# First-layer eviction as tanh(h/2) under activation tables that also hold arctan or sine, with every step handed over in a new order

## The chip, the cores and the metric

The kernel runs on one core of one Trainium2 chip. The metric is the device time of one execution in microseconds (us). The core has five engines that run side by side and wait for one another through semaphores: TensorE (PE, with its weight loads as PEld), VectorE (DVE), ScalarE (ACT), GpSimd (POOL) and SyncE (SP), which here only issues DMAs. Each engine works through its own list of instructions in the order in which the program handed them over; an instruction that waits holds back all that stand behind it on its engine.

## The reference

Three layers follow one another. The first is a linear recurrence with decay over 768 steps (4 batches, 8 heads, head size 48), the second a feed-forward layer with the activation h·tanh(softplus(h)), the third eight experts with a greedy assignment of 3072 tokens.

```python
for t in range(S):                       # recurrence
    cur = einsum('bhd,bhe->bhde', u * kt, vt)
    y[:, :, t] = einsum('bhd,bhde->bhe', rt, state + cur)
    state = wt[..., None] * state + einsum('bhd,bhe->bhde', kt, vt)
...
h = x @ w_in                             # 384 -> 2048
g = h * tanh(log1p(exp(h)))
x = g @ w_out                            # 2048 -> 384
...
logits = x @ w_gate                      # greedy: best (token, expert) first, 384 tokens each
h = maximum(x[mask] @ w1[e], 0.0); out[mask] = h @ w2[e]
```

The kernel uses that, with s = sigmoid(−h), tanh(softplus(h)) = sin(pi/2 − 2·arctan(s)): first s, then its arctan, then a sine with scale −2 and bias pi/2.

## The kernel before, in words

The first two layers run interleaved, in 12 groups of 256 tokens. Two attention units (128 tokens each; 24 in all, numbered n) make the input `xg` of one group. Group g of the second layer has eight slots: slot t (96 in all, 8g to 8g+7) is one `mm1`, 18 matmuls into one of two PSUM buffers `Hp`, followed by its eviction on ScalarE (L579, into `es`) and a scaled copy of h (L348, into `hs`; L348 is the helper `move` when it goes to ScalarE, L346 when it goes to VectorE). After four slots, half a group H = 2g or 2g+1 is complete: `act_ln` takes the arctan of the half in one instruction (L588), `act_sin` the sine in two (L597), `act_he` multiplies by h on VectorE (L605), and `act_g` writes the result as a high and a low f16 part (the high by `move`, the low on VectorE, L622). The second matmul, `mm2` (L636), takes g from there; it runs as one stream of 384 steps of three matmuls for the 12 groups, far behind `mm1`, and `CFG["rate"]` and `CFG["beat"]` say how many steps are handed over at each slot. When a tile's 16 steps end, `put_x1` takes it out of PSUM and a DMA writes it away.

An attention unit has ten steps: `att0` (a running product on VectorE and a product `rk`), `att_inv` (Ln and Exp on ScalarE, L376 and L377), `att1` and `att1b` (four products on VectorE, L384 to L416), `bon1` and `bon2` (small matmuls, their evictions, and `Dt`), `att_K` (transposes and the copy `kn`), `att_A` (64 small matmuls), `att_S` (the state; L467 and L472 to L476) and `att4` (the output y: 32 matmuls, the high part of `xg` by `move`, the low part on VectorE, L496). After the second unit of a group, six DMAs on SyncE's queue (L502) bring the last rows of `xg` in place.

The weights of the second layer are converted from f64 to two f16 halves by the kernel itself in the first 16 slots (`conv` and `split`, VectorE and ScalarE; `og_T` and `og_M` fold the gate's weights in). After the last slot come the gate (VectorE, with the rest of the `mm2` stream as filler on TensorE) and the experts.

The order is written out by hand. Every step is put on a list with a key (`at(key, step)`); the list is sorted by key and handed over in that order, and each engine works in that order. Slot t has key t + `CFG["mm1"]`; the steps of a unit have keys `8*(n//2) - 8` plus the offsets of `CFG["u"]`. `CFG["dve"]` says which of the movable instructions go to VectorE. The functions of ScalarE belong to named sets of tables, and the trace has a load (ACT_TABLE_LOAD, 1283 ns) wherever the next function is of another set; copies run without one. `natural_log_exp_and_others` (Ln and Exp) is loaded before `att_inv` and `trig_and_small` (arctan and sine) before the arctan and sine of both halves of a group, each by a call; the load for the sigmoid of the next eviction is put in by the framework. In groups 1 to 10 ("both" in the code), the Ln and Exp of two units, the arctan of the odd half and all four sines stand one behind another at the start of the next group, ahead of that group's first eviction.

Of the kernel before, what the change touches and what calls it, by code (L numbers as in the profile page):

```python
# [18 lines left out]
P = 128  # L19
# [4 lines left out]
CFG = {'conv': [-27.9, -26.2, -0.2, 0.8, 1.8, 2.8, 3.7, 5.3, 5.9, 6.6, 7.3, 8.0, 8.7, 10.4, 10.6, 11.3],  # L24
 'split': [-27.3, -25.6, 0.9, 1.9, 2.9, 3.8, 4.7, 5.6, 6.7, 7.4, 8.1, 8.8, 9.0, 11.2, 11.4, 12.1],
 'ogT': [7.4, 8.45, 9.9, 10.25, 10.95, 11.85, 12.55, 12.75],
 'ogM': [8.15, 9.35, 10.2, 10.9, 11.35, 11.95, 12.75, 13.95],
 'u': ({'att0': -5.0, 'bon1': -3.1, 'bon2': -2.1, 'inv': 0.1, 'r1': 0.101, 'k1': 0.102, 'K': 1.28, 'A1': 1.3,
        'S': 2.39, 'y': 2.4},
       {'att0': -2.8, 'bon1': -1.9, 'bon2': -0.8, 'inv': 0.11, 'r1': 0.111, 'k1': 0.112, 'K': 3.3, 'A1': 3.4,  # L30
        'S': 4.59, 'y': 4.6}),
 'un': {0: {'att0': -17.25,
            'inv': -16.75,
            'r1': -16.55,
            'bon1': -15.85,
            'k1': -16.37,
            'K': -16.05,
            'A1': -15.25,
            'bon2': -15.45,
            'S': -15.75,  # L40
            'y': -13.75},
        1: {'att0': -20.15,
            'inv': -20.14,
            'r1': -19.9,
            'bon1': -19.0,
            'k1': -19.4,
            'K': -17.4,
            'A1': -17.4,
            'bon2': -18.5,
            'S': -17.0,  # L50
            'y': -17.15},
        2: {'att0': -19,
            'inv': -18.99,
            'r1': -18.9,
            'bon1': -17.98,
            'k1': -18.85,
            'bon2': 4.5,
            'K': 5.3,
            'A1': 5.5,
            'S': 5.5,  # L60
            'y': 7.4},
        3: {'att0': -22.95,
            'inv': -22.8,
            'r1': -17.6,
            'bon1': 2.3,
            'k1': -17,
            'bon2': 3.05,
            'K': 3.85,
            'A1': 4.2,
            'S': 4.05,  # L70
            'y': 6.5},
        4: {'K': 4.96,
            'A1': 4.82,
            'S': 6.99,
            'y': 7.0,
            'att0': -0.0,
            'bon1': 0.87,
            'bon2': 3.15,
            'inv': 2.57,
            'r1': 2.6,  # L80
            'k1': 3.2},
        5: {'y': 7.46,
            'att0': -1.5,
            'bon1': 2.0,
            'bon2': 4.6,
            'inv': 3.67,
            'r1': 3.7,
            'k1': 4.3,
            'K': 5.9,
            'A1': 6.2,  # L90
            'S': 7.45},
        6: {'att0': -3.6, 'bon1': -2.7, 'bon2': -0.9},
        7: {'att0': -1.4, 'bon1': -0.6, 'bon2': -0.4}},
 'rate': [(9, 0), (16, 19), (80, 195), (82, 200), (85, 216), (89, 218), (93, 234), (99, 258)],
 'beat': (16, 80, (5, 3, 2, 2, 2, 2, 1, 5)),
 'close_cv': 15.0,
 'close_att': 86.65,
 'mm1': 0.7,
 'mm2': 1.275,
 'aln': -0.1,  # L100
 'tanh': (1.475, 1.66),
 'g': (3.0, 3.0725),
 'both': ((0.12, (0.14, 0.15), (1.33, 2.75)), (0.13, (2.45, 2.5), (3.6, 4.7))),
 'begin': {('warm', 0): -32,
           ('wg',): 5.6,
           ('ld', 4): -23.99,
           ('ld', 5): -25.98,
           ('ld', 6): -23.8,
           ('ld', 7): -21.7,
           ('ld', 8): -23.6,  # L110
           ('ld', 9): -23.6,
           ('warm', 1): -25.1,
           ('warm', 2): -24.4,
           ('warm', 3): 0.15,
           ('warm', 4): 5.65,
           ('warm', 5): 7.15,
           ('warm', 6): 9.9},
 'warm': [36, 12, 18, 12, 12, 0, 12],
 'amount': {'I0': 3, 'I1': 0, 'g': 1, 't': 6, 'c': 3, 'o': 11},
 'dve': {'lg': set(),  # L120
         'glo': {0,
# [51 lines left out]
         'ghi': {2} | {i for i in range(4, 46) if i % 4 != 3},  # L173
         'hs': set(),
         'rk': {0, 1, 2, 3, 5, 6, 7, 9, 10, 11, 12, 13, 14, 15, 16, 17, 18, 19, 20, 21, 22, 23},
         'x0': set(),
         'bT': {22},
         'wT': {4}},
 'nd0': 8,
 'lg2': 5.2,  # L180
 'alone': {9},
 'lg': 4.9,
# [4 lines left out]
def tile_rwkv_mish_greedy_moe(  # L187
# [111 lines left out]
    nc.scalar.preload_act_table_set("natural_log_exp_and_others")  # L299
# [9 lines left out]
    nc.vector.memset(right, math.pi / 2)  # L309

# [42 lines left out]
    def warm(n):  # L353
        if n:
            wps = pq.tile([P, 512], F32, name="Y", bufs=2)
        for _ in range(n):
            nc.tensor.matmul(wps, id16, warm_rhs, start=True, stop=True)
# [13 lines left out]
    def att_inv(n):  # L371
        need(("att0", n))
        inv = pa.tile([P, 2 * NP, L], F32, name="inv", bufs=2)
        if n > 1 and (n < 6 or n % 2 == 0):
            nc.scalar.preload_act_table_set("natural_log_exp_and_others")
# [22 lines left out]
    def bon2(n):  # L398
        pb = pq.tile([P, C], F32, name="Y", bufs=2)
        nc.tensor.transpose(pb, bTs.pop(n), ident)  # L400
# [21 lines left out]
    def att_A(n):  # L422
        c = UN[n][1]
        need(("k1", n), *([("S", n - 1)] if c else []))
        made.add(("A", n))
        k1, r1, _ = st[n]
# [16 lines left out]
    def att_K(n):  # L443
        need(("k1", n))
        k1, r1, _ = st[n]
        if UN[n][1] + 1 < NCH:
            t = pq.tile([P, NP, C], F32, name="Y", bufs=2)
            for p in range(NP):
                nc.tensor.transpose(t[:, p, :], k1[:, p, :], ident)
# [132 lines left out]
    def act_ln(H_):  # L582
# [3 lines left out]
        if H_ % 2 and 0 < H_ // 2 < NG - 1:  # L586
            nc.scalar.preload_act_table_set("trig_and_small")
# [739 lines left out]
```

## Time and profile before

| | |
|---|---|
| time, median of 3 runs | 871.36 us (871.22 to 871.53) |
| the profiled execution's own time | 869.97 us |
| its span, first to last instruction | 868.3 us |
| TensorE matmuls busy | 757.0 us, 87% of the span |
| VectorE / ScalarE / GpSimd busy | 542.5 / 456.4 / 63.8 us |
| mean granted clock of TensorE | 0.965 of full speed |
| loads of function tables on ScalarE | 44, 1283 ns each |

The profile lists, for each stretch or instruction, when it began, how long it took, the engine, the line of the kernel, and in brackets how long the engine had stood idle before it and what ended that. `x18` counts instructions merged into one row. A matmul's duration holds a tail that overlaps the next one; the distance from one row's start to the next is what it costs TensorE.

### The profile page before, as it was taken

The page shows a single profiled execution, that of the slowest core. Times are in us where ns is not written, and L with a number is a line of the kernel's source. Part 1 is how long each engine was busy: PE and PEld are TensorE (multiplying, and loading weights), DVE is VectorE, ACT ScalarE, POOL GpSimd, SP SyncE. Part 2 cuts the span into 40 slices and gives each one's busy share as a digit, 9 for nine tenths or more (in the row PEclk, how much of TensorE's full clock was granted, in tenths as well). Part 3 has the DMA queues.
Part 4 walks back from the last instruction along what each step waited for, and adds up shares of the span by engine and source line. Part 5 has one row for each costly group of instructions (what it writes and reads, how often), then busy time and mean ns, then how long its engine had stood idle before and what let it go on. Part 6 is the DMA issues. An engine that isn't in the chain of part 4 may idle for free. (4 is left out here: it accounts for less than half of the span.)

```text
span 868.3 us, 20153 instructions
## 1 busy us (share of the span) xinstructions
PE 757.0 (87%) x8819; PEld 521.7 (60%) x8819; DVE 542.5 (62%) x949; ACT 456.4 (53%) x682; POOL 63.8 (7%) x102
## 2 busy tenths in 40 slices
PE   6763879898989989898898878999959999999996
PEld 3452656676767767676676656555536566555564
DVE  7699884958668584967667243577765433555520
ACT  2358885775848666674748376411005543455521
POOL 1000000000000000000000001000011331222311
PEclk9797899999999999999999999999979999999999
DMA  7860512304121240322200000400144445554200
GB/s 281 246 187 14 147 37 53 75 14 89 40 59 39 52 83 6 88 49 52 45 18 11 15 10 11 164 20 20 30 160 147 145 143 182 191 191 166 79 29 28
DMA packets 22220, 74.12 MB, mean 85 GB/s; under 512 B 4496, under 2 KB 13072, under 8 KB 20080
## 3 DMA queue, kind: packets, MB, share of 16 engines
q1 hardware_dynamic: 19056, 63.35, 25.1%
q0 software_dynamic: 3072, 9.44, 3.4%
q8 instruction: 71, 1.16, 0.6%
q14 instruction: 21, 0.17, 0.1%
HBM read 62.15 MB, written 9.44 MB: 82 GB/s over the span
## 5 line engine op out<-in xcount | busy, mean ns | idle before, releaser
L576 PE MATMUL Hp<-xg,wi 128*128 128x256 f16 x1728 | 211.3, 278 | 12.4 <-ACT hs L348 10.7
L636 PE MATMUL X<-wo,g 128*128 128x392 f16 (+1 forms) x1152 | 214.6, 330 | 0.5 <-ACT wT L348 0.5
L576 PEld LDWEIGHTS <-wi 128*128 128x128 f16 x1728 | 169.1, 100 | 42.9 <-issue 11.1
L636 PEld LDWEIGHTS <-g 128*128 128x128 f16 x1152 | 107.5, 99 | 64.1 <-issue 1.7
L579 ACT ACTIVATE es<-Hp 128x512 f32<-128x512 f32 x96 | 57.4, 598 | 131.0 <-PE Hp L576 130.9
L1172 PE MATMUL Hp<-xe,a 128*128 128x384 f16 (+1 forms) x612 | 100.8, 316 | 6.5 <-DVE hT L1177 5.2
L1189 PE MATMUL X<-a,hT 128*128 128x384 f16 x576 | 97.2, 326 | 0.0
L1172 PEld LDWEIGHTS <-a 128*128 128x128 f16 x612 | 57.6, 98 | 48.3 <-issue 14.4
L1189 PEld LDWEIGHTS <-hT 128*128 128x128 f16 x576 | 56.4, 98 | 34.8
L605 DVE TENSOR_TENSOR hs<-hs,es 128x1024 f32<-128x1024 f32 x48 | 56.7, 1220 | 29.8 <-ACT es L597 29.8
L622 DVE TENSOR_TENSOR g<-hs,g 128x1024 f16<-128x1024 f32 x48 | 58.6, 1225 | 22.4 <-ACT g L348 21.3
L1177 DVE SCALAR_TENSOR_TENSOR hT<-Hp,hT 128x384 f16<-128x384 f32 x64 | 35.4, 554 | 46.8 <-ACT hT L1176 46.8
L1118 DVE SCALAR_TENSOR_TENSOR a<-stg,a 128x1024 f16<-128x1024 f32 (+4 forms) x56 | 59.6, 1066 | 3.2 <-ACT a L1115 2.7
L348 ACT ACTIVATE hs<-Hp 128x512 f32<-128x512 f32 x96 | 57.1, 595 | 0.0
L1115 ACT ACTIVATE a<-stg 128x1024 f16<-128x1024 f32 (+4 forms) x56 | 51.1, 926 | 6.3 <-DMA stg<-in_w_dram 6.3
L1192 ACT ACTIVATE or<-X 128x384 f32<-128x384 f32 x24 | 11.8, 491 | 81.0 <-issue 60.7
L597 ACT ACTIVATE es<-es,right 128x1024 f32<-128x1024 f32 x48 | 51.4, 1135 | 0.1
L1154 DVE SCALAR_TENSOR_TENSOR xe<-cn,xe 128x384 f16<-128x384 f32 x24 | 13.3, 555 | 60.7 <-ACT xe L1153 60.7
L1176 ACT ACTIVATE hT<-Hp 128x384 f16<-128x384 f32 x64 | 31.4, 491 | 32.9 <-PE Hp L1172 31.8
L348 ACT ACTIVATE x1o<-X 128x384 f32<-128x384 f32 x19 | 9.3, 491 | 71.3 <-issue 60.1
L588 ACT ACTIVATE es<-es 128x2048 f32<-128x2048 f32 x24 | 45.9, 1914 | 0.1
L412 DVE TENSOR_TENSOR E<-inv,E 128x512 f32<-128x512 f32 x23 | 15.9, 692 | 40.5 <-ACT inv L377 39.2
(194 smaller groups left out, 904.4 us busy)
## 6 DMA issues: line engine op xcount, KB each, us to landing
stg<-in_w_dram SPq DMA_DIRECT2D x16, 1536.0 KB, 7.2
T<-in_rkw_dram SPq DMA_DIRECT2D x42, 289.5 KB, 5.0
v<-in_v_dram SPq DMA_DIRECT2D x24, 192.0 KB, 3.9
raw<-in_w_out_dram SPq DMA_DIRECT2D x6, 768.0 KB, 4.7
x_dram<-x1o SPq DMA_DIRECT2D x48, 96.0 KB, 2.2
wo<-in_w_in_dram SPq DMA_DIRECT2D x4, 768.0 KB, 8.0
raw<-in_w_in_dram SPq DMA_DIRECT2D x2, 768.0 KB, 7.7
g<-in_w_in_dram SPq DMA_DIRECT2D x2, 768.0 KB, 10.4
```

The costliest lines, as they stand in the source:

```text
L348: nc.scalar.activation(dst, src, AF.Copy, scale=scale)
L576: nc.tensor.matmul(h[:, fi, :], wi[:, a, kk, f * P:(f + 1) * P], xg[g][:, b, kk, :], start=(n == 0), stop=(n == 3 * KD - 1))
L579: nc.scalar.activation(es[g, hf][:, 2 * q:2 * q + 2, :], h, AF.Sigmoid, scale=-1.0 / (SX * SWI))
L588: nc.scalar.activation(e, e, AF.Arctan)
L597: nc.scalar.activation(e, e, AF.Sin, scale=-2.0, bias=right)
L605: nc.vector.tensor_tensor(h, h, e, op=ALU.mult)
L622: (nc.vector if on_v("glo", 2 * H_ + q) else nc.gpsimd).tensor_tensor(gt[:, 1, sl], h, gt[:, 0, sl], op=ALU.subtract)
L636: nc.tensor.matmul(x, gt[:, a, ff, m * P:(m + 1) * P], wo[:, b, f, 0:n], start=(f == 0 and i == 0), stop=(f == NF - 1 and i == 2))
L1115: nc.scalar.activation(dst[:, 0], src, AF.Copy, scale=sc_)
L1118: nc.vector.scalar_tensor_tensor(dst[:, 1], src, sc_, dst[:, 0], op0=ALU.mult, op1=ALU.subtract)
L1172: nc.tensor.matmul(ps[:, cs], a1[:, a, kk, f * P:(f + 1) * P], x[:, b, kk, cs], start=(n == 0), stop=(n == 3 * KD - 1))
L1189: nc.tensor.matmul(ps, h[:, a, f, ms], a2[:, b, f, :], start=(n == 0), stop=(n == 3 * NF2 - 1))
```

## The change

1. The eviction of the first layer (L579) is tanh(h/2) in place of sigmoid(−h). The arctan is then taken of 0.5 − 0.5·tanh(h/2), by scale and bias of that instruction, with the bias 0.5 in a new [128, 1] tile `mid_`.
2. A helper `tables(*sets)` remembers which set is loaded and loads the first of the sets named only if none of them is. Ln and Exp ask for the log set; the tanh for `sigmoid_and_others` or `silu_and_others`; the arctan for the first of these or the trigonometric set; the sine for the second or the trigonometric set.
3. Arctan, sines, `act_he` and `act_g` of every group, the first and the last two among them, are placed by one table of offsets, `CFG["half"]`, from the key 8·(h//2)+8.
4. All keys change, and so does what goes to VectorE (`CFG["dve"]`: 13 of the 14 copies `kn` and 21 of the 33 high parts of g go over to ScalarE; 20 copies `hs`, 11 high parts of `xg`, 7 copies of `mm2` results and a few small ones to VectorE) and the number of `mm2` steps per slot.
5. Bookkeeping of which `Y` or `X` tile of PSUM was taken last (`"whole"`) asserts an order while the program is built; it issues nothing.

Worked out from the keys, the order around the border of two groups (from slot 47 to slot 51; "x7" counts `mm2` steps) is

```
before: mm1 47 | inv 14, inv 15, arctan 11, sines of 10 and 11 | mm2 x5, mm1 48 | mm2 x5, K 14, A 14, mm1 49 | mm2 x3 ...
after:  y 13, bon1 15, mm1 47 | arctan 11, sines of 10 and 11 | mm2 x7, mm1 48 | mm2 x9 | inv 14, inv 15 | mm1 49 | mm2 x3, K 14, A 14, mm1 50, mm1 51 ...
```

and `mm2` steps per group of eight slots are 21 in place of 22 between slots 16 and 80; both orders have handed over 258 at the end. The y of a group's second unit stands ahead of slot 7 of the group before, in place of slot 4. The number of table loads in the program falls from 44 to 37; in a group between slots 16 and 80 it stays at three.

```diff
-        if n > 1 and (n < 6 or n % 2 == 0):
-            nc.scalar.preload_act_table_set("natural_log_exp_and_others")
+        tables(LOG)
...
+    table = [None]
+
+    def tables(*sets):
+        if table[0] not in sets:
+            table[0] = sets[0]
+            nc.scalar.preload_act_table_set(sets[0])
+
+    LOG, TAN, SIN, TRIG = "natural_log_exp_and_others", "sigmoid_and_others", "silu_and_others", "trig_and_small"
...
-        nc.scalar.activation(es[g, hf][:, 2 * q:2 * q + 2, :], h, AF.Sigmoid, scale=-1.0 / (SX * SWI))
+        tables(TAN, SIN)
+        nc.scalar.activation(es[g, hf][:, 2 * q:2 * q + 2, :], h, AF.Tanh, scale=0.5 / (SX * SWI))
...
-        if H_ % 2 and 0 < H_ // 2 < NG - 1:
-            nc.scalar.preload_act_table_set("trig_and_small")
-        nc.scalar.activation(e, e, AF.Arctan)
+        tables(TAN, TRIG)
+        nc.scalar.activation(e, e, AF.Arctan, scale=-0.5, bias=mid_)
...
-            if q == 0 and not both:
-                nc.scalar.preload_act_table_set("trig_and_small")
+            tables(SIN, TRIG)
             nc.scalar.activation(e, e, AF.Sin, scale=-2.0, bias=right)
...
+        t0 = 8 * (h // 2) + 8
+        o = {**CFG["half"][h % 2], **CFG["halves"].get(h, {})}
+        at(t0 + o["at"], act_ln, h)
+        for q in range(2):
+            at(t0 + o["sin"][q], act_sin, h, q)
+            at(t0 + o["he"][q], act_he, h, q)
+            at(t0 + o["g"][q], act_g, h, q)
...
- 'beat': (16, 80, (5, 3, 2, 2, 2, 2, 1, 5)),
+ 'beat': (16, 80, (9, 3, 0, 0, 2, 0, 0, 7)),
...
+ 'half': ({'at': -2.795, 'sin': (-0.016, -0.015), 'he': (0.269, 0.464), 'g': (1.712, 3.088)},
+          {'at': -0.109, 'sin': (0.379, 0.536), 'he': (0.613, 1.164), 'g': (3.652, 5.128)}),
...
- 'u': ({'att0': -5.0, 'bon1': -3.1, 'bon2': -2.1, 'inv': 0.1, 'r1': 0.101, 'k1': 0.102, 'K': 1.28, 'A1': 1.3,
-        'S': 2.39, 'y': 2.4},
-       {'att0': -2.8, 'bon1': -1.9, 'bon2': -0.8, 'inv': 0.11, 'r1': 0.111, 'k1': 0.112, 'K': 3.3, 'A1': 3.4,
-        'S': 4.59, 'y': 4.6}),
...
-         'kn': {5, 11, 17, 19, 23, 6, 8, 10, 12, 14, 16, 18, 20, 22},
-         'x1': {2, 3, 5, 7, 8},
-         'ghi': {2} | {i for i in range(4, 46) if i % 4 != 3},
-         'hs': set(),
...
-         'x0': set(),
...
+         'kn': {16},
+         'x1': {2, 3, 4, 5, 6, 7, 8, 10, 14, 16, 20, 22},
+         'ghi': {33, 4, 37, 5, 9, 13, 45, 17, 21, 25, 29, 31},
+         'hs': {10, 20, 21, 23, 28, 31, 39, 44, 47, 52, 55, 60, 63, 68, 71, 76, 79, 87, 92, 95},
...
+         'x0': {1, 5, 8, 9, 11, 13, 15, 17, 19, 21, 23},
```

The new offsets of a unit of the steady part (after; first and second unit of a group) are: `att0` −3.415 and −1.479, `bon1` −2.42 and −0.473, `bon2` −0.705 and −0.017, `inv` 1.465 and 1.625, `r1` 1.47 and 1.642, `k1` 1.491 and 1.961, `K` 2.416 and 5.074, `A1` 2.578 and 5.44, `S` 3.86 and 6.027, `y` 3.922 and 6.883.

## Rows read from the trace of the kernel before

**Rows 1.** Stages: us of the stretch, then each engine's busy time, granted clock.

```profile
44.18:110.00 65.82, 41.40 (x661) 31.95 (x656) 61.83 (x90) 47.55 (x70) 1.38 (x1) 0.88 0.38 110
110.00:146.58 36.58, 30.42 (x461) 23.59 (x460) 24.80 (x39) 22.53 (x39) 1.26 (x1) 0.97 0.19 48
146.58:456.09 309.51, 275.19 (x4077) 210.31 (x4075) 216.59 (x318) 207.24 (x297) 1.04 (x1) 0.99 0.23 50
456.09:551.05 94.96, 82.77 (x890) 59.20 (x888) 43.99 (x61) 60.98 (x77) 2.38 (x16) 0.96 0.07 15
```

**Rows 2.** What TensorE waited for, 146.58 to 456.09: total us, times, longest.

```profile
PE Y L467 <- DVE kn L346: 12.8, 10, 3.9
```

**Rows 3.** Timeline of TensorE over one group: start, us, what, idle before.

```profile
223.33 2.13 PE L576 MATMUL Hp<-xg,wi 128*128 128x256 f16 x18
...
233.76 0.68 PE L467 MATMUL Y<-v,kn 64*64 64x48 f32 x32 [0.73 <-DVE kn L346]
...
235.73 2.13 PE L576 MATMUL Hp<-xg,wi 128*128 128x256 f16 x18 [0.66 <-ACT hs L348]
...
244.52 0.67 PE L489 MATMUL A<-Dt,v 64*48 64x64 f32 x32 [1.52 <-DVE Dt L440]
...
252.37 0.43 PE L394 MATMUL Y<-rk,u_T 128*32 128x64 f32 x16 [1.58 <-DVE rk L368]
...
258.28 2.65 PE L636 MATMUL X<-wo,g 128*128 128x392 f16 x15
260.77 2.13 PE L576 MATMUL Hp<-xg,wi 128*128 128x256 f16 x18
```

**Rows 4.** Timeline of ScalarE at the border of two groups.

```profile
259.58 1.28 ACT L375 ACT_TABLE_LOAD   x1
...
263.37 1.28 ACT L587 ACT_TABLE_LOAD   x1
264.67 1.92 ACT L588 ACTIVATE es<-es 128x2048 f32<-128x2048 f32 x1
266.48 4.25 ACT L597 ACTIVATE es<-es,right 128x1024 f32<-128x1024 f32 x4
...
270.74 1.28 ACT L579 ACT_TABLE_LOAD   x1
272.03 0.60 ACT L579 ACTIVATE es<-Hp 128x512 f32<-128x512 f32 x1
```

**Rows 5.** Groups of instructions, whole span: busy us, mean ns, idle before.

```profile
L622 DVE TENSOR_TENSOR g<-hs,g 128x1024 f16<-128x1024 f32 x48 | 58.6, 1225 | 22.4 <-ACT g L348 21.3
L348 ACT ACTIVATE g<-hs 128x1024 f16<-128x1024 f32 x15 | 15.7, 1057 | 0.3 <-DVE hs L605 0.3
L416 DVE SCALAR_TENSOR_TENSOR T<-inv,T 128x512 f32<-128x512 f32 x24 | 16.6, 692 | 0.8
```

**Rows 6.** The way of `xg`: timeline of VectorE and SyncE, and its DMAs' landing.

```profile
246.21 0.75 DVE L496 SCALAR_TENSOR_TENSOR xg<-A,xg 128x256 f16<-128x256 f32 x2
247.03 4.82 SPq L502 DMA_DIRECT2D xg<-xg  x6
...
DMA to landing us min/median/max: 1.8/1.9/7.5
```

**Rows 7.** End of the interleaved part: timeline, and two waits of TensorE, 456.09 to 551.05.

```profile
510.57 3.38 PE L576 MATMUL Hp<-xg,wi 128*128 128x256 f16 x18 [4.53 <-ACT hs L348]
539.92 1.91 ACT L588 ACTIVATE es<-es 128x2048 f32<-128x2048 f32 x1
546.68 2.36 DVE L622 TENSOR_TENSOR g<-hs,g 128x1024 f16<-128x1024 f32 x2
551.05 0.35 DVE L892 TENSOR_REDUCE wk<-V 128x1 f32<-128x192 f32 x1
...
PE Hp L663 <- ACT g L348: 3.3, 3, 1.5
PE Y L467 <- DVE kn L346: 2.2, 1, 2.2
```

More of the change, by code (lines that the diff above doesn't have):

```diff
@@ L96 @@
  'close_cv': 15.0,
  'close_att': 86.65,
[L98 to L104, printed above, removed]
+ 'mm1': 0.724,
+ 'mm2': 1.324,
+ 'half': ({'at': -2.795, 'sin': (-0.016, -0.015), 'he': (0.269, 0.464), 'g': (1.712, 3.088)},
+          {'at': -0.109, 'sin': (0.379, 0.536), 'he': (0.613, 1.164), 'g': (3.652, 5.128)}),
+ 'halves': {},
+ 'begin': {('warm', 0): -33.78,
@@ L105 @@
            ('wg',): 5.6,
-           ('ld', 4): -23.99,
+           ('ld', 4): -25.706,
            ('ld', 5): -25.98,
-           ('ld', 6): -23.8,
+           ('ld', 6): -24.091,
            ('ld', 7): -21.7,
            ('ld', 8): -23.6,
[L111 to L118, printed above, removed]
+           ('ld', 9): -23.974,
@@ L119 @@
+           ('warm', 1): -24.946,
+           ('warm', 2): -24.041,
+           ('warm', 3): -1.989,
+           ('warm', 4): 4.794,
+           ('warm', 5): 9.244,
+           ('warm', 6): 9.808},
+ 'warm': [37, 12, 14, 20, 15, 2, 8],
  'amount': {'I0': 3, 'I1': 0, 'g': 1, 't': 6, 'c': 3, 'o': 11},
  'dve': {'lg': set(),
-         'glo': {0,
[51 rows of a table removed]
-         'ghi': {2} | {i for i in range(4, 46) if i % 4 != 3},
-         'hs': set(),
-         'rk': {0, 1, 2, 3, 5, 6, 7, 9, 10, 11, 12, 13, 14, 15, 16, 17, 18, 19, 20, 21, 22, 23},
@@ L176 @@
-         'x0': set(),
-         'bT': {22},
-         'wT': {4}},
+         'glo': {0, 1, 2, 3, 4, 5, 6, 7, 8, 9, 10, 11, 12, 13, 14, 15, 16, 17, 18, 19, 20, 21, 22, 23, 24, 25, 26, 27,
[5 rows of a table added]
+         'ghi': {33, 4, 37, 5, 9, 13, 45, 17, 21, 25, 29, 31},
[5 rows of a table added]
  'nd0': 8,
- 'lg2': 5.2,
[1 row of a table added]
  'alone': {9},
- 'lg': 4.9,
+ 'lg': 7.167,
  'hold': 30}
@@ L309, in tile_rwkv_mish_greedy_moe @@
     nc.vector.memset(right, math.pi / 2)
+    mid_ = const.tile([P, 1], F32, name="mid_")
+    nc.vector.memset(mid_, 0.5)
     wi = pm.tile([P, 2, KD, FF], F16, name="wi")
@@ L355, in warm @@
             wps = pq.tile([P, 512], F32, name="Y", bufs=2)
+        made.add("whole")
         for _ in range(n):
@@ L373, in att_inv @@
         inv = pa.tile([P, 2 * NP, L], F32, name="inv", bufs=2)
[L374 to L375 removed]
+        tables(LOG)
         nc.scalar.activation(inv, E_of(n)[:, :, 1:], AF.Ln)
@@ L399, in bon2 @@
         pb = pq.tile([P, C], F32, name="Y", bufs=2)
+        made.add("whole")
         nc.tensor.transpose(pb, bTs.pop(n), ident)
@@ L425, in att_A @@
         made.add(("A", n))
+        made.discard("whole")
         k1, r1, _ = st[n]
@@ L447, in att_K @@
             t = pq.tile([P, NP, C], F32, name="Y", bufs=2)
+            made.add("whole")
             for p in range(NP):
@@ L478, in att4 @@
     def att4(n):
-        need(("A", n))
+        need(("A", n), "whole")
         made.add(("y", n))
@@ L535, in og_T @@
         need(("w", NS + f // 2))
+        made.add("whole")
         ps = pp.tile([P, 2, KD, P], F16, name="X", bufs=2)
@@ L568, in mm1 @@
             hs[g, hf, q // 2] = pm.tile([P, NF // 4, G], F32, name="hs", bufs=5)
-        made.add(("mm1", g, hf, q))
+        made.update((("mm1", g, hf, q), "whole"))
         h = pp.tile([P, 2, G], F32, name="Hp", bufs=2)
@@ L632, in mm2_part @@
         x = xps[g, m][:, 0:n]
+        made.add("whole")
         gt = gs[g, f // (NF // 2)]
@@ L773, in tile_rwkv_mish_greedy_moe @@
     for h in range(NSLOT // 4):
-        t = 4 * h + 4
-        both = 0 < h // 2 < NG - 1
-        at(t + (0.115 if both and h % 2 else CFG["aln"]), act_ln, h)
-        if both:
-            t0 = 8 * (h // 2) + 8
-            sin, he, g = CFG["both"][h % 2]
-            at(t0 + sin, act_sin, h, 0, 1)
-            for q in range(2):
-                at(t0 + he[q], act_he, h, q)
-                at(t0 + g[q], act_g, h, q)
-        else:
-            for q in range(2):
-                at(t + CFG["tanh"][q], act_tanh, h, q)
-                at(t + CFG["g"][q], act_g, h, q)
+        t0 = 8 * (h // 2) + 8
[5 more added lines that the diff above has]
+            at(t0 + o["g"][q], act_g, h, q)
+        t = 4 * h + 4
         if h % 2 and ND0 <= h // 2 < NG - 1:
```

158 lines of the change are left out of this document (88 added, 70 removed), and 56 rows, old and new, of the table CFG.

## The prediction

> **What bounds the kernel now.** I read first the table of stages, with each engine's busy time, then what TensorE waited for, then the timelines of TensorE and ScalarE over one group, the grouped instructions for durations, and the chain that ended last. The last lies wholly in the experts, which the change does not touch; so the question is how much earlier they can begin, at the end of a part in which the first two layers are interleaved. [rows 1] split that part in four. From 44.18 to 110 VectorE is busy 61.83 of 65.82 us and sets the pace (it converts weights). From 110 on TensorE is the busiest: 275.19 of 309.51 us in the eight groups of slots 16 to 79, 82.77 of 94.96 in the two groups behind them up to the gate. No other engine is over 70% in the eight groups, so their length is TensorE's work plus the time in which its ordered list stands still.
>
> One group shows how much that is. Its first slot starts at 223.33, the next group's at 260.77: 37.44 us. In it TensorE waits four times: for a copy `kn` on VectorE (0.73), for an eviction (0.66), for `Dt` (1.52) and for `rk` (1.58), in all 4.49 [rows 3]. Its own work is thus 32.95 us. The mean of the eight groups is 309.51/8 = 38.69, because some have a longer wait for `kn`: 12.8 us in ten waits, 3.9 the longest [rows 2].
>
> Where these waits come from is seen on ScalarE at the border of two groups [rows 4]. A load at 259.58, Ln and Exp of two units (2.5 us), a load, the arctan (1.8 to the next start), four sines (4.26), a load, and only at 272.03 the next eviction: 12.45 us in which no first-layer result leaves PSUM and all that VectorE and TensorE get from ScalarE comes late.
>
> **The change part by part.** *Table loads.* The program has 7 fewer (37 against 44), 7 x 1.28 = 9.0 us of ScalarE [rows 4]; all seven are outside the eight groups, where it stays at three for each. ScalarE has room there (207 of 309.5 us busy, [rows 1]), so I count nothing for them by themselves. What the new sets do is to cut the 12.45 us in two: arctan and sines stand ahead of the next slot's eviction, Ln and Exp behind it.
>
> What the row shows of a load is 1.28 us, and Ln starts right after it [rows 4]. The Trainium skill, "ScalarE: Activation LUTs", section "What ACT_TABLE_LOAD costs", gives about 2.66 us for a switch, a drain of 1.38 included; by that the three loads of a group would be 8.0 us in place of 3.9, before and after alike. The trace has no such drain behind a load.
>
> *ScalarE at the border, new order.* I count from the end of a group's last mm1. Eviction of it 0.1 to 0.6 (its `hs` is on VectorE in most groups); arctan, now with a bias tile, 1.9; load 1.3; sines 4.26: to 8.05. Eviction of slot 0 of the next group 1.0: 9.05. Load 1.3, Ln and Exp of the first unit 1.25: 11.6; of the second: 12.85; a high part of g (1.0, [rows 5]): 13.85; load: 15.15; eviction of slot 1: 16.15. VectorE turns the first unit's result into k with three products of 0.69 [rows 5]: 13.7.
>
> *TensorE at the same time.* 7 steps of `mm2` at 0.5 (5 in 2.49 us, [rows 3]): 3.5; slot 0, 2.0: 5.5; 9 steps: 9.95; slot 1: 11.9; 3 steps: 13.4, where it wants that k (13.7 and a semaphore): a wait of 0.4. Slot 3, which needs the buffer of slot 1, begins after `K`, `A` and slot 2, past 17, and the buffer is free at 16.15: no wait. So the wait for evictions (0.66 here) is gone, those for `kn` too (it now runs on ScalarE behind evictions that are on time), and `Dt`'s (1.52), since in the new order two slots lie between `A` and y.
>
> *The rest of the group.* The movable instructions: 13 `kn` and 21 high parts go to ScalarE, some 30 others to VectorE; per group both engines change by about 1 us, ScalarE to some 27 us and VectorE to some 28 (an estimate from their 207 and 217 us over eight groups, [rows 1]). Late in the group VectorE has the second unit's state, then a running product and `rk` for the unit after next, and TensorE meets `bon1` about 0.4 us before `rk` is there (it was 1.58, [rows 3]).
>
> *A new wait.* The y of a group's second unit now stands ahead of slot 7, not slot 4, so the way of `xg` gets short. From y's end VectorE needs about 0.5 (what stands ahead), 0.7 (the high part, a 512-column step as L416) and 0.75 (the low part), then SyncE issues six DMAs 0.8 us apart, and the last lands 1.9 us after its issue [rows 5, 6]: 1.95 + 4.0 + 1.9 = 7.85 us. TensorE has `bon1` (0.4), its wait (0.4), slot 7 (2.0), small ones (0.2) and 7 steps (3.5) = 6.5 before the next group's slot 0. That is a stall of 1.35 if the first matmul waits for all six DMAs, 0.65 if each third of them waits for its own; the old order never showed it, with four slots in between. I take 1.2, the higher end, as one semaphore may cover all. Behind slot 0 on TensorE's list stand the 9 steps and slot 1, and ScalarE's eviction at 8.05 still finds slot 0 done (5.5 + 1.2), so it goes no further.
>
> *The group.* 32.95, less one `mm2` step in a group (21 for 22, 0.5) = 32.45; plus 0.4 + 0.4 + 1.2 = 34.45. For waits that come only in some groups I add 0.8: before, the mean stood 1.25 over the group that I read. 35.25 x 8 = 282.0, against 309.51: **−27.5 us**.
>
> *Slots 80 to 95.* The steps put off are made up here: 59 steps of `mm2` in place of 52 before the last slot, +3.5. Against that go the wait of 4.53 for an eviction at 510 (with silu's set the tanh needs no load behind the sines, and 12 steps cover them) and the slow slot behind it (3.38 for 2.13, [rows 7]), three waits of the logits for g (3.3; they now come two slots after it), and 2.2 for `kn` [rows 7]: −11.3. Sum −7.8.
>
> *The end.* Here the change loses. Before, the first half of the last group was through when its second half's arctan began at 539.92; the last low part ended at 549.04, 9.1 later, and the gate began at 551.05 [rows 7]. Now all four sines stand behind that arctan: 1.9 + 1.3 + 1.06 to the first, then four products and four low parts at 1.2 and a high part at 0.6 on VectorE: 14.1. TensorE has 18 steps (9 us) beside it and then waits. **+5.0**, and with the line above −2.8.
>
> *The head.* VectorE's list sets it [rows 1], and has the same conversions. Some copies go to it (about +3 us), a few idle places go as arctan and sines move back and loads fall away. I take −2, and −6 and +4 as its ends.
>
> **Sum.** −27.5 − 2.8 − 2.0 = −32.3. From the profiled execution's own 869.97 (its span of 868.3 and 1.7 around it) that is 837.7. The median of the runs is 871.36, 1.4 above it; so 839.1.
>
> **The rivals.**
>
> *More than that.* If no wait but 0.65 for `xg` is left, a group takes 33.1, eight 264.8 (−44.7), and with −7 and −4 for end and head the time is about 816. For it: no engine but TensorE has 85% of a group.
>
> *VectorE takes over.* Between the first unit's Exp (11.6) and the last piece of `xg`, its new list has 14 steps of about 0.69, six of about 1.22 (running products counted so), two low parts at 0.75 and two state updates of about 1.1: 20.7 us of some 22 [rows 5, 6]. A little late help from ScalarE (four high parts of g a group, three of them now its own) makes it the bound; at 2 us more a group: +16, about 855.
>
> *Slower, through `xg`.* The same lateness goes one to one into the wait of slot 0 for `xg`, as the six DMAs leave only after VectorE's last piece. The gain of 32.3 over eight groups is 4.0 a group: if VectorE reaches the second unit's y more than 4 us later than I count (some 4.5 in place of 0.5 ahead of it), the kernel is slower than before. At 5.2 us late: +41.6, about 880. Against it: TensorE itself waits less for VectorE the later it runs, and VectorE still has idle time while the sines run.
>
> *Only the number of loads counts.* Where a set is switched as often as before, splitting the border would bring nothing, and only the loads that are gone, 9.0 us at most, could show, some of them beside other waits: about 864. This is what the Trainium skill ("ScalarE: Activation LUTs", "Table sets: the hidden batching unit") asks for, calls batched by set and all of one set before the next, and the new order spreads them. The rows speak against it: of 37.44 us, 4.49 are waits of an ordered list, and none ends in a load.
>
> *The sets don't do it.* If tanh after a sine still took a load, ScalarE's way at the border would be 1.3 longer, k and slot 3 as late, +10: about 849.
>
> **How the numbers follow.** Forecast 0.58 (own range 828 to 850), more 0.15, VectorE 0.13, slower 0.07, loads only 0.04, sets 0.03. The range takes in VectorE's case and the upper part of the better one: 819 to 862. A difference of 0.2% is about what a measurement of this kernel can tell from none. Faster by over that 0.90; within it, mostly where lateness of VectorE just eats the gain, 0.03; slower 0.07.
>
> **What would show it.** Right: the eight groups near 282 us, waits for `rk`, `Dt`, `kn` and evictions of 1 us a group in all, a wait of slot 0 for `xg` of about 1, three loads a group with the sines' load ahead of slot 0's eviction and the log set's behind it, no wait at 510, and some 5 us of idle TensorE before the gate. Wrong: groups over 36 us with VectorE over 85% busy; a wait for `xg` over 3; loads in front of a tanh that follows a sine; a head longer than before.

## The result, and the profile after

The changed kernel takes 838.6 us (median of four runs, 836.1 to 840.8) against 871.3 of the kernel before beside it: ratio 0.963, 95% interval 0.959 to 0.967, **faster by 3.7%**. The forecast was 839.1. The profiled execution took 836.1, its span is 834.4.

Stages after: the stretch, then for each engine busy time and instructions, then the granted clock of TensorE (the last two numbers are the share of its DMA engines and GB/s). The borders answer to those of [rows 1].

```profile
44.89:111.34 66.45, 49.22 (x667) 35.77 (x662) 60.52 (x92) 41.34 (x62) 0.00 (x0) 0.82 0.36 103
111.34:149.31 37.97, 30.47 (x447) 23.41 (x444) 25.04 (x39) 22.79 (x39) 0.00 (x0) 0.96 0.19 49
149.31:427.52 278.21, 267.86 (x4047) 205.19 (x4045) 219.66 (x328) 212.76 (x287) 0.00 (x0) 0.99 0.25 55
427.52:515.40 87.88, 84.44 (x916) 60.74 (x916) 44.08 (x64) 62.71 (x78) 2.38 (x16) 0.96 0.14 43
515.40:834.40 319.00, 295.29 (x2253) 178.56 (x2251) 165.36 (x394) 100.34 (x172) 54.58 (x72) 0.97 0.32 107
```

With the fourth stretch cut where the last arctan starts (539.92 before, 497.56 after), by spans:

| stage | before | after | change | forecast |
|---|---|---|---|---|
| head, up to slot 16's `mm2` | 146.58 | 149.31 | +2.7 | −2.0 |
| slots 16 to 79, eight groups | 309.51 | 278.21 | −31.3 | −27.5 |
| slots 80 to 95, up to the last arctan | 83.83 | 70.04 | −13.8 | −7.8 |
| last arctan to the gate | 11.13 | 17.84 | +6.7 | +5.0 |
| gate and experts | 317.25 | 319.00 | +1.8 | 0 |
| sum | 868.3 | 834.4 | −33.9 | −32.3 |

What TensorE waited for in the eight groups after (us in total, times, longest):

```profile
PE Y L433 <- DVE T L398: 5.9, 6, 3.0
PE Y L375 <- DVE rk L350: 2.8, 7, 0.9
PE Hp L561 <- DMA xg<-xg: 1.4, 2, 0.8
```

That is 10.1 us. The same view of before sums to 34.1: 12.8 for `kn` [rows 2], and

```profile
PE Y L394 <- DVE rk L368: 11.0, 7, 1.6
PE Hp L576 <- ACT hs L348: 6.1, 6, 1.2
PE A L489 <- DVE Dt L440: 2.4, 3, 1.5
```

with 1.8 in three small ones. So 24.0 of the 31.3 us are waits that are gone. Another 5.0 are second-layer steps that now stand elsewhere (492 matmuls for 522 in the stretch, nine steps of three in 4.48 us). The remaining 2.3 us are about what `mm1` gives, whose 1154 matmuls are busy 136.6 us for 139.6.

ScalarE at the border of two groups after, to be held against [rows 4]:

```profile
256.57 1.28 ACT L275 ACT_TABLE_LOAD   x1
257.86 4.26 ACT L580 ACTIVATE es<-es,right 128x1024 f32<-128x1024 f32 x4
262.03 0.60 ACT L565 ACTIVATE es<-Hp 128x512 f32<-128x512 f32 x1
...
263.14 1.28 ACT L275 ACT_TABLE_LOAD   x1
264.43 0.63 ACT L357 ACTIVATE inv<-E 128x512 f32<-128x512 f32 x1
...
267.87 1.28 ACT L275 ACT_TABLE_LOAD   x1
```

Slot 0's eviction at 262.03 follows the sines with no load between, and Ln and Exp come behind it. TensorE at the same border (start, us, what, idle before):

```profile
257.24 2.13 PE L561 MATMUL Hp<-xg,wi 128*128 128x256 f16 x18
259.21 4.64 PE L616 MATMUL X<-wo,g 128*128 128x392 f16 x27
...
267.96 0.66 PE L433 MATMUL Y<-ident,T 128*128 128x128 f32 x4 [0.65 <-DVE T L398]
...
285.71 0.43 PE L375 MATMUL Y<-rk,u_T 128*32 128x64 f32 x16 [0.34 <-DVE rk L350]
```

Slot 0, 9 steps, slot 1 and 3 steps (left out), then a wait for k: the forecast order. From the sines' load at 256.57 to the next group's at 290.90 it is 34.33 us.

The way of `xg` in that group (VectorE's low parts, SyncE's six issues), and the end:

```profile
286.20 0.76 DVE L480 SCALAR_TENSOR_TENSOR xg<-A,xg 128x256 f16<-128x256 f32 x2
287.02 4.02 SPq L486 DMA_DIRECT2D xg<-xg  x6
```

```profile
497.09 9.10 PE L616 MATMUL X<-wo,g 128*128 128x392 f16 x54
...
508.48 1.64 PE L643 MATMUL Hp<-g,wo 128*8 128x256 f16 x36 [1.86 <-DVE g L327]
...
512.39 2.10 PE L616 MATMUL X<-wo,g 128*128 128x384 f16 x6
514.29 0.86 PE L655 MATMUL Hp<-pick,lgt 128*128 128x8 f32 x4
```

TensorE runs its 18 steps beside the sines, then waits 1.86 us, and 0.82 and 0.75 in two more pieces, 3.4 in all, for the last parts of g; after them six matmuls take 2.10 us and the sum of the logits 0.86.

### The profile page after: what moved, and what is told of

Same layout as the page of the kernel before. It is cut to its first block, busy times and chain, and to the rows that moved or that the text cites. A ratio compares the mean times of both kernels' runs of the same rounds, so it can differ in the third digit from the quotient of the medians.

```text
span 834.4 us, 20144 instructions
## 1 busy us (share of the span) xinstructions
PE 762.4 (91%) x8825; PEld 523.3 (63%) x8825; DVE 548.4 (66%) x971; ACT 452.8 (54%) x658; POOL 58.7 (7%) x98
## 5 line engine op out<-in xcount | busy, mean ns | idle before, releaser
L616 PE MATMUL X<-wo,g 128*128 128x392 f16 (+1 forms) x1152 | 210.9, 332 | 0.6 <-ACT wT L329 0.6
L1146 PEld LDWEIGHTS <-a 128*128 128x128 f16 x612 | 57.7, 98 | 48.4 <-issue 14.5
L329 ACT ACTIVATE x1o<-X 128x384 f32<-128x384 f32 x12 | 5.8, 485 | 80.4 <-PE X L616 53.0
L573 ACT ACTIVATE es<-es,mid__121 128x2048 f32<-128x2048 f32 x24 | 48.0, 2000 | 0.3
L329 ACT ACTIVATE hs<-Hp 128x512 f32<-128x512 f32 x76 | 45.0, 592 | 0.0
```

Source lines behind the costliest of these rows:

```text
L329: nc.scalar.activation(dst, src, AF.Copy, scale=scale)
L573: nc.scalar.activation(e, e, AF.Arctan, scale=-0.5, bias=mid_)
L616: nc.tensor.matmul(x, gt[:, a, ff, m * P:(m + 1) * P], wo[:, b, f, 0:n], start=(f == 0 and i == 0), stop=(f == NF - 1 and i == 2))
L1146: nc.tensor.matmul(ps[:, cs], a1[:, a, kk, f * P:(f + 1) * P], x[:, b, kk, cs], start=(n == 0), stop=(n == 3 * KD - 1))
```

## The experiments

Times are medians; a ratio is to the kernel before, run on the same chip, where its median was 869.6 to 871.4. "The changed kernel" is 838.6.

**The order without the sets.** The eviction is a sigmoid again, everything else as changed.

```diff
-        tables(TAN, SIN)
-        nc.scalar.activation(es..., h, AF.Tanh, scale=0.5 / (SX * SWI))
+        tables(TAN)
+        nc.scalar.activation(es..., h, AF.Sigmoid, scale=-1.0 / (SX * SWI))
```

> The changed kernel's order, movable sets and timings, but the first layer's eviction is a sigmoid again, in a table of its own: each group goes LOG, table, trig, table, so eight table loads of 1.28 us come back in the groups of slots 16 to 79 and ScalarE's list grows by 1.3 us per group (212.8 to about 223 us of the 278 us stretch). Theory (the sets matter only where a load stands ahead of something that TensorE waits for; here the fourth load is ahead of LOG and tan work that sets the time of k): about 1.2 us per group, +8 to +12 us on the changed kernel, about 849. Rival 1 (the order alone makes the gain, ScalarE has room): within 2 us of the changed kernel, 837 to 841. Rival 2 (the sets alone make the gain): back to 865 or more.

855.5, ratio 0.983 (0.981 to 0.985): 16.9 slower than the changed kernel, all in the groups (294.70 us, +16.5). The 8 to 12 that were expected are right in kind and too small. The extra load puts Ln 1.40 later (7.97 us from the sines' load to that of Ln, for 6.57). The wait for k grows from 5.9 to 16.7. The rest, 5.7 us, is as much as the busy time of `mm1` grows with TensorE's clock: 142.3 us for 136.6. Two groups of this run, the same wait and then the same two slots:

```profile
311.33 0.66 PE L433 MATMUL Y<-ident,T 128*128 128x128 f32 x4 [1.89 <-DVE T L398]
...
313.01 5.77 PE L561 MATMUL Hp<-xg,wi 128*128 128x256 f16 x36
```

```profile
348.64 0.66 PE L433 MATMUL Y<-ident,T 128*128 128x128 f32 x4 [1.89 <-DVE T L398]
...
350.32 4.10 PE L561 MATMUL Hp<-xg,wi 128*128 128x256 f16 x36
```

The granted clock is 0.83 from 307 to 317 and 1.00 from 347 to 357: part of the first pair of slots ran at 1.2 GHz, the second at 2.4. Four of the eight groups went the first way.

**The sets without the order.** The kernel before, with tanh and the same function that asks for a set only where it is needed.

```diff
+        tables(TAN, SIN)
-        nc.scalar.activation(es..., h, AF.Sigmoid, scale=-1.0 / (SX * SWI))
+        nc.scalar.activation(es..., h, AF.Tanh, scale=0.5 / (SX * SWI))
```

> The order, movable sets and timings of the kernel before, but evictions as tanh, with the tables asked for only where the resident one lacks the function. In the old order evictions stand between ln/exp and arctan and behind the sines, so the loads per group stay at three or four; what changes is which of them come ahead of an eviction. Theory (sets without the new order move nothing, or next to nothing): 868 to 873, at most 3 us under the kernel before. Rival (the sets bring the gain by themselves, TensorE no longer waits for the loads ahead of evictions): 845 to 860.

892.2, ratio 1.025 (1.023 to 1.027): 21 slower than before. Both expectations missed. In the old order one half's arctan comes after the sines, and the sines' set has none:

```profile
236.04 1.28 ACT L304 ACT_TABLE_LOAD   x1
...
252.22 1.28 ACT L304 ACT_TABLE_LOAD   x1
253.51 2.00 ACT L597 ACTIVATE es<-es,mid__121 128x2048 f32<-128x2048 f32 x1
```

The load at 252.22 is a fourth one in the group; and arctan and sines no longer share a set (the load at 236.04 stands between them, where [rows 4] has none). The waits for `kn` grow from 12.8 to 22.3. So neither order nor sets is worth 33 us by itself: alone the sets cost 21, and the order with its moved copies gives 16.

**The movable copies, both ways.** First the changed kernel with the old sets of what runs on VectorE, then the old kernel with the new sets.

```diff
- 'dve': { ... 'kn': {16}, 'ghi': {33, 4, 37, ...}, 'rk': {0, 1, ...}, ... }
+ 'dve': { ... 'kn': {5, 11, 17, 19, ...}, 'ghi': {2} | {...}, 'rk': {0, 1, 2, 3, 5, ...}, ... }
```

> The changed kernel with one part undone: the sets that say which copies and high parts go to VectorE or ScalarE are those of the kernel before (k's transposed copy and high parts partly on VectorE, rk and more copies on the engines that they had). Theory (the new sets unload VectorE, which is 79% busy in slots 16 to 79, so that k and the low parts come in time): waits for VectorE's T and low parts come back at 1 to 2 us per group, +8 to +16 us, 847 to 855. Rival (the sets only follow the new order and are worth nothing by themselves): within 2 us of the changed kernel, 837 to 841.

851.1, ratio 0.977 (0.975 to 0.979): 12.5 slower than the changed kernel, within the range. The groups take 292.57, and TensorE's waits there sum to 22.4, two of the largest being

```profile
PE Y L479 <- DVE T L444: 9.9, 7, 3.0
...
PE Y L479 <- DVE S L504: 4.0, 5, 0.8
```

VectorE's busy time in the groups is lower here than in the changed kernel (216.4 for 219.7 us). So the new sets do not pay by unloading VectorE, as the expectation had it; what comes late is its products (`T`, `rk`) and its state (`S`), at the moment when TensorE asks for them.

> The kernel before with one part of the change alone: the movable copies and high parts stand on the engines that the changed kernel has them on (kn on ScalarE but for one unit, rk and most other small copies on VectorE); order, sets and eviction are the old ones. Theory (the movable sets pay only with the new order, in which evictions are on time and ScalarE has room ahead of kn): the wait for kn (12.8 us in the eight groups) turns into one for ScalarE behind the tables of the border, within 6 us of the kernel before, 865 to 877. Rival (the movable sets carry the gain, since they take kn off VectorE): 10 us or more faster than before, under 861.

883.7, ratio 1.015 (1.014 to 1.017): 14 slower than before, the theory in kind, at over twice its size. The wait for `kn` did change its engine, and those for `rk` (7.5) and `Dt` (5.3) stay (150.29 to 467.0, the eight groups):

```profile
PE Y L421 <- ACT kn L302: 20.1, 7, 3.9
```

Behind a border of 12.45 us [rows 4] ScalarE is no better a place for `kn`: its wait is 20.1 us for 12.8. The prediction had tied its move to evictions that are on time, and this run bears that out; but it had no price for the moved copies, and with the new order they are worth 12.5. Both runs move all the copies together, so what `kn` alone does is not shown.

**The end.** The first half of the last group as before: its sines and products ahead of the last arctan, under the set that holds both.

```diff
- 'halves': {},
+ 'halves': {22: {'at': -3.93, 'sin': (-3.92, -3.91), 'he': (-3.9, -3.89), 'g': (-1.9, -0.9)}},
-        tables(TAN, TRIG)
+        tables(*((TRIG,) if H_ == NSLOT // 4 - 2 else (TAN, TRIG)))
```

> The changed kernel with the last two halves' order as in the kernel before: the first half's arctan, sines and high and low parts ahead of the last half's arctan, under the table that holds both. Theory (the stretch from the last arctan to the gate's first VectorE step is 17.8 us because the first half's two sines of 2.1 us stand between; before it was 11.1): it falls by 5 to 6.5 us, and the whole by about 5 to 6, to 832 to 834. Rival (the end is bound by the last half's own chain and by TensorE's second layer, the sines only fill): within 1.5 us of the changed kernel.

831.9, ratio 0.955 (0.954 to 0.957): 6.7 less than the changed kernel by the medians, 4.3 by the profiles, where the stretch from the last arctan to the gate is 13.53 for 17.84:

```profile
508.54 1.05 PE L643 MATMUL Hp<-g,wo 128*8 128x256 f16 x32 [0.66 <-ACT g L329]
...
510.21 1.15 PE L616 MATMUL X<-wo,g 128*128 128x384 f16 x6
511.19 0.51 PE L655 MATMUL Hp<-pick,lgt 128*128 128x8 f32 x4
```

The waits are 1.1 us for 3.4, and without the long ones the six matmuls take 1.15 for 2.10 and the sum 0.51 for 0.86: 1.3 us of clock (granted 1.00 in this stretch for 0.82).

**Is VectorE next?** Two multiplications of 0.7 us more in each group, once early, once late.

```diff
+        if H_ % 2 == 0 and q == 0 and 1 <= H_ // 2 <= 8:      # early, ahead of hs * es
+            for _ in range(2):
+                nc.vector.tensor_tensor(first, first, first, op=ALU.mult)
+        if m == 1 and 3 <= g <= 10:                           # late, behind y's low parts
+            for _ in range(2):
+                nc.vector.tensor_tensor(first, first, first, op=ALU.mult)
```

> The changed kernel with two VectorE multiplications more (128x520, about 0.7 us each, of a constant with itself) in each of the eight groups, put ahead of the group's first product with a sine, where VectorE idles 1.77 us. Theory (VectorE's position in a group decides, not its busy share): they fit into that idle time, 0 to +0.3 us per group, 0 to +2 us in all, 837 to 842. Rival (VectorE, 79% busy in this stretch, has become the bound or next to it): +0.8 to 1.4 us per group, +6 to +11 us, as much as in the run with the same two instructions late in the group.

838.1, ratio 0.964 (0.961 to 0.967): nothing, as expected.

> The changed kernel with the same two VectorE multiplications in each of the eight groups, now behind the low part of the second unit's y, late in the group, where VectorE makes bt, Dt and bT for the transposes that TensorE meets just ahead of the group's last steps of the second layer. Theory (late in the group VectorE is 0.1 to 0.4 us ahead of TensorE): the transposes wait, +1.0 to +1.4 us per group, +8 to +11 us, 846 to 850. Rival (VectorE is idle a fifth of the time, so 1.4 us are absorbed wherever they stand): within 2 us of the changed kernel.

838.9, ratio 0.964 (0.963 to 0.966): nothing either, where 8 to 11 us were expected. New waits did come, in three of the eight groups, and another shrank: that for k is 4.7 us in all here, for 5.9.

```profile
PE Y L382 <- DVE bT L327: 3.2, 3, 1.1
```

Where a wait of about 1 us came, the wait for k behind it is gone, and the group is longer by 0.3 to 0.6 only (34.88 and 34.81 us from one group's sines to the next, where the changed kernel has 34.30 and 34.51). So little of what TensorE meets late in a group reaches the group's length.

**Filling the wait for k.** One step of the second layer moved to where TensorE idles.

```diff
- 'beat': (16, 80, (9, 3, 0, 0, 2, 0, 0, 7)),
+ 'beat': (16, 80, (9, 4, 0, 0, 2, 0, 0, 6)),
```

> The changed kernel with one step of the second layer moved in each group: 9, 4, 2, 6 in place of 9, 3, 2, 7, so that a step of 0.5 us stands where TensorE now waits 0.65 us (3.0 in the first group) for k. Theory (that wait is idle time which a step can fill): -0.4 to -0.5 us per group, about -4 us, 833 to 836. Rival (the six steps left ahead of the next group's slot 0 no longer cover the way of xg, whose last DMA lands when that slot is under way): the wait moves there, and the time stays within 1 us of the changed kernel.

840.6, ratio 0.967 (0.963 to 0.970): no gain. The wait for k goes from 5.9 to 0.8, that for `xg` from 1.4 to 3.5, and the first group runs out of finished g (us in total, times, longest):

```profile
PE X L616 <- DVE g L327: 4.2, 1, 4.2
PE Hp L561 <- DMA xg<-xg: 3.5, 7, 1.5
...
PE Y L433 <- DVE T L398: 0.8, 4, 0.2
```

That looked like a loop through `xg`. So the step was moved from slot 24 on, and in every group three of the six DMAs went to another queue:

```diff
-                    nc.sync.dma_start(x[...], x[...])
+                    (nc.gpsimd if j else nc.sync).dma_start(x[...], x[...])   # or nc.scalar
```

> The changed kernel with the step of the second layer moved as in the run that moved one (9, 4, 2, 6), from slot 24 on, so that the first group, which ran out of steps there, keeps 9, 3, 2, 7; and three of the six DMAs that bring xg together go out on GpSimd's queue beside three on SyncE's. Theory (a group's length is set by one loop: Ln and Exp, k, the attention steps, xg's DMAs, slot 0; moving the step alone only moved the idle time from k to xg): with the last DMA issued some 2 us earlier (4.0 to 4.8 us for six on one queue) the moved step counts, -0.5 us in seven groups, 833 to 836 us, and the wait for xg falls under 1 us in all. Rival 1 (xg's way is not what the moved step ran into, or GpSimd's DMAs land no earlier): the xg wait of 0.4 to 0.5 us per group stays, 837 to 841. Rival 2 (GpSimd's DMAs cost VectorE or land later): slower, over 842.

837.8, ratio 0.963 (0.961 to 0.965), for the 833 to 836 of the theory: no gain that can be told. The DMAs do leave earlier, in 2.0 us instead of 4.0, and no wait for `xg` is left; but the wait for k is back, at 6.6:

```profile
284.59 1.96 SPq L486 DMA_DIRECT2D xg<-xg  x3
...
285.09 1.49 POOL L486 DMA_DIRECT2D xg<-xg  x3 [32.78 <-DVE bt L327]
```

The loop through `xg` falls: neither it nor the steps that cover it on TensorE set the length. The four regular groups take 34.3 to 34.5 us in the changed kernel, with the moved step, and with the two queues.

> The same as the run with three of xg's DMAs on GpSimd's queue, but with those three on ScalarE's queue, where the issuing takes some 2 us of ScalarE's time while it idles 1.0 to 2.6 us ahead of slot 7's eviction. Theory: the last DMA lands as early as on GpSimd's queue or earlier, -0.5 us in seven groups, 833 to 836; but slot 7's eviction, the arctan and the sines behind it come some 0.7 us later, which a free 1 us ahead of slot 0's eviction should take. Rival (ScalarE's list is in the loop at this place too): k comes 0.7 us later, +0.2 to +0.7 us per group, 839 to 845.

850.3, ratio 0.976 (0.974 to 0.978): the rival, with more than its price of 839 to 845. In the profiled execution 5 us of it are there before the groups begin (slot 10 starts at 116.37 for 111.34), and in the groups the waits of TensorE are 17.3 us for 10.1. The issue stands ahead of slot 7's eviction on ScalarE:

```profile
294.31 1.91 ACTq L486 DMA_DIRECT2D xg<-xg  x3
296.26 0.60 ACT L565 ACTIVATE es<-Hp 128x512 f32<-128x512 f32 x1 [3.35 <-PE Y L382]
```

**The loop.** What the runs have in common is one number, the time from the sines' load to the transposes of the first k (`K`):

| kernel | sines' load | `K` starts | between | next sines' load | group |
|---|---|---|---|---|---|
| changed | 256.57 | 267.96 | 11.39 | 290.90 | 34.33 |
| step moved, two queues | 288.47 | 299.83 | 11.36 | 322.77 | 34.30 |
| sigmoid, new order | 227.06 | 239.85 | 12.79 | 261.27 | 34.21 |
| sigmoid, three groups on | 335.84 | 348.64 | 12.80 | 371.70 | 35.86 |

(The group from 227.06 is the one that has k for one unit only.) Slot 7's eviction, arctan, load, four sines, slot 0's eviction, load, Ln, Exp, k: in these groups none of that waits for TensorE once slot 7 is done. The rest of the group, from `K` to the next sines' load, is TensorE's list up to slot 7, 22.94 us in the first two rows. If this sets the length, then taking two sines out of it must shorten the group, even at the price of a fourth load.

```diff
- 'halves': {},
+ 'halves': {h: {'sin': (-2.41, -2.409)} for h in 2, 4, ..., 20},
-        tables(TAN, SIN)
+        tables(*((TAN,) if j == NS - 1 and 0 < g < NG - 1 else (TAN, SIN)))
```

> The changed kernel with ScalarE's list alone altered; TensorE's and VectorE's lists keep their order. In the groups that end at slots 16 to 88 the first half's two sines (2.13 us) run right behind the first half's arctan, ahead of slot 5's eviction, under a load of their own, and the load back for the second half's arctan stands ahead of slot 7's eviction, where ScalarE idles 2.6 us. So a group has four table loads in place of three, but between slot 7's eviction and the one of slot 0 stand two sines and not four. Theory (a group's length is set by a loop on ScalarE and VectorE: slot 7's eviction, arctan, load, sines, slot 0's eviction, load, Ln, Exp, k; the beat run and the two-queue run showed that neither the moved step nor the way of xg sets it): k comes 2.1 us earlier, the wait for it goes (0.65 per group, 3.0 to about 1 in the first), the regular group falls from 34.3 to 33.4 to 33.7 us, 5 to 8 us in all with the clock, 831 to 834. Rival 1 (the number of loads is what counts, as a fourth load cost 17 us with sigmoid): +8 us or more, over 846. Rival 2 (VectorE or rk sets the group's length, k comes earlier and the wait moves to rk): 836 to 840.

836.6, ratio 0.960 (0.958 to 0.962). That misses the 831 to 834, lies in the range of the rival that moves the wait to `rk`, and is not told from the changed kernel by the time alone. By the trace the loop holds in the regular groups:

```profile
286.61 1.28 ACT L275 ACT_TABLE_LOAD   x1
...
288.56 0.60 ACT L565 ACTIVATE es<-Hp 128x512 f32<-128x512 f32 x1 [0.67 <-PE Hp L561]
...
291.21 1.28 ACT L275 ACT_TABLE_LOAD   x1
```

The wait for k is gone from every group but the first (0.9 in all), and three regular groups take 33.54 to 33.59 us (the first of them from the sines' load at 291.21 to the next at 324.75), where the answering ones of the changed kernel took 34.30 to 34.51; 33.4 to 33.7 were expected. What is left of waits in a regular group is 0.34, for `rk`, so of the 2.1 us only 0.75 count: then TensorE's own work is the bound. Other places give much of it back. The first group has a wait of 2.5 for `rk`, and the group with k for one unit only takes 34.43 for 32.97, with waits of 1.0 for `xg` and 0.9 for an eviction; the eight take 275.54 for 278.21. In slots 80 to 95 a copy on ScalarE comes 1.8 us late.

**Both together**, the end and the sines:

> Two edits on the changed kernel together: the first half's sines behind its own arctan in the groups that end at slots 16 to 88 (a fourth load, but a shorter way from slot 7's eviction to k), and the last group in the order of the kernel before, first half through ahead of the second half's arctan under the table that holds both. Theory (the two act in different stages and add): 6.5 us from the end as in its own run (831.9), and 5 to 8 us from the groups, 824 to 828. Rival (the sines' edit gives nothing or costs): 830 to 834, or above.

829.8, ratio 0.953 (0.951 to 0.955): under both kernels, 8.8 below the changed one and 2.1 below the run with the end alone. It misses the 824 to 828: the end counts in full, but the sines bring 2 us in place of 5 to 8, with the same wait of 2.5 in the first group and of 1.8 in slots 80 to 95.

## Why the prediction was right, step by step

The mechanism was right in the groups. That the sum of the spans, −32.3, lies 1.6 us from the measured −33.9 is in part luck: the groups (by 3.8) and slots 80 to 95 (by 6.0) gained more than forecast, while the head (by 4.7), the end (by 1.7) and the part behind it (by 1.8) lost more.

**The border and the groups.** The mechanism is as told: no waits for evictions, `Dt` or `kn`, three loads a group with the sines' ahead of slot 0's eviction and Ln's behind it. Its size, −27.5 for −31.3, is made of errors that partly cancel.
- *TensorE's own work*, 32.45 in the sum, is 33.5 ((278.21 − 10.1)/8). The group that I read has `K` and the state for one of its two units only: four transposes and 32 products with `kn` where seven of the eight groups have eight and 64. One such group in after (223.60 to 256.57) takes 32.97, a regular one 34.33. The 0.8 that I added "for waits that come only in some groups" stands for no wait; by luck it covers most of this work.
- *The wait for k*: 0.4 forecast, 0.65 in a regular group, 3.0 in the first; mean 0.74. *`rk`*: 0.4 forecast, 0.35.
- *`xg`*: 1.2 forecast, 0.18 measured. The way itself was right: low parts end at 286.96, six issues take 4.02 and the last lands about 1.8 later, near 292.9, while slot 0 starts at 291.66. But each third of its matmuls waits for its own DMAs. I had both prices, 0.65 and 1.35, and took the wrong end; the measured wait is below both.

**Loads by themselves.** Counting nothing was right for three against three (24 in the eight groups before and after), and a fourth shows why: with sigmoid it lies in the loop and k comes 1.40 later, one load of 1.28 and little more; in the sines' run it lies where ScalarE idles, and the group gets shorter by 0.75. The Trainium skill, "ScalarE: Activation LUTs", section "What ACT_TABLE_LOAD costs", with about 2.66 us for a switch, is not borne out by that 1.40. The Trainium skill's section "Table sets: the hidden batching unit" on the same page counts switches; here one switch more in each group cost 16.9 us in one place and nothing that can be told in another.

**Rivals.** *More than that* falls with the eight groups at 278.2 us, where it had 264.8: TensorE's own work alone is 268. *VectorE takes over* falls: 219.66 of 278.21 us busy, and 1.4 us more in each group cost nothing that can be told, early or late. *Only the number of loads* falls with −31.3 in the groups at the same three loads. *The sets don't do it* came out on the chip as the sigmoid run, 855.5 for the 849 of the rival: there I had left out what the waits do to the clock. *Slower through `xg`*: its waits were 1.4 us in all.

**Slots 80 to 95**, −13.8 for −7.8. Of the 11.3 that I listed, 10.0 were waits and 1.25 a slow slot. The waits of this stretch were 11.6 and all are gone; TensorE is busy for the whole 70.04. The steps put off added 16 matmuls, 2.7 us, not 3.5. What is then left, about 4.8 us, goes with the clock, before 0.96 and in after 1.00, and I had counted only the 1.25: `mm1` alone takes 34.1 us (288 matmuls) for 36.5 (290).

**The end**, +6.7 for +5.0. The work was sized right: the last low part ends 14.5 us after the arctan starts. The terms that I named add up to just that; the 14.1 was a slip, and without it the forecast would have been +5.4. Left out: after its waits TensorE runs the logits' sum and six matmuls slowly, and the run with the old end shows 1.3 us of that.

**The head**, +2.7 for −2.0, is the step that failed in sign, and a longer head was one of the signs of being wrong that I had named. Up to slot 10 nothing changed (111.34 for 111.17): there the run with the old movable sets starts at 109.19, so the moved copies cost 2.2 us (about 3 forecast) and the rest of the change gave back only 2.0 of the 5 that my −2 needs. Then, first before, second after,

```profile
115.73 0.49 PE L539 MATMUL X<-id,wo 128*128 128x128 f16 x6 [1.29 <-ACT wT L348]
116.07 1.66 PE L636 MATMUL X<-wo,g 128*128 128x392 f16 x9
```

```profile
116.12 0.49 PE L524 MATMUL X<-id,wo 128*128 128x128 f16 x6 [2.32 <-ACT wT L329]
116.45 3.09 PE L616 MATMUL X<-wo,g 128*128 128x392 f16 x9
```

In the new order a high part of g (1.05 us) stands ahead of `wT` on ScalarE, and TensorE has less to do ahead of it. The wait was 1.29 and becomes 2.32, which by itself makes the matmuls start only 0.4 later; but the 9 matmuls behind it take 3.09 for 1.66 (granted clock from 116 to 120: 0.57, before 1.00), and that 1.4 is half of the head's +2.7. A new wait of 0.77 for `rk` follows at 145.21, where before there was one of 0.46 for `bT`. I had weighed the head by VectorE's list alone, which sets the pace only to 110. With the old movable sets the head ends 1.0 earlier (148.34); the rest I did not separate.

**Gate and experts**, +1.8 for 0. The same instructions at a granted clock of 0.97 for 0.98; 604 to 664 has 0.86 where the answering stretch before has 0.89. Why is open; no run was made for it.

## What to carry to other kernels

When an ordered list stands still, look for the loop that sets the period and not for the engine that waits. Here the loop of a regular group ran from slot 7's eviction through ScalarE to k, and on TensorE's list back to slot 7; filling the wait (two runs) left the group's length as it was, and taking 2.1 us out of the loop shortened it by 0.75, although it added a table load. Order, tables and the places of copies were one change: the tables alone and the places alone made the kernel 21 and 14 us slower, the order and the places without the new tables gave half of the gain. And a group that is read as the pattern must be checked for its counts against the mean of all.

## What was not expected of the hardware

A wait of TensorE cost more than its length here, and not always the same. After two equal waits of 1.89 us two slots took 5.77 us in one group and 4.10 in another; what decides between them is not shown. The same spread separates executions: in the late run, whose first 119 us follow those of the changed kernel within 0.25 us, the granted clock from 120 to 135 is 0.77 where the changed kernel's was 1.00, and slot 16's `mm2` comes 2.6 us later.

```profile
120.00:135.00 15.00, 11.27 (x111) 8.56 (x110) 8.89 (x14) 7.54 (x15) 0.00 (x0) 0.77 0.01 1
```

```profile
120.00:135.00 15.00, 10.58 (x186) 8.91 (x184) 9.19 (x15) 9.62 (x18) 0.00 (x0) 1.00 0.01 3
```

The first row is of the late run, the second of the changed kernel (the clock is the number after POOL's). The difference is of the size of the 4.7 us between the lowest and the highest run of the changed kernel; that it is their cause was not shown.
